# One reduction in place of three adds behind the attention's products with v, and another order of the work

## The chip, the cores and the metric

The kernel runs on one core of a Trainium2 chip. The metric is the device time in microseconds of one execution. TensorE (PE) does the matrix products, VectorE (DVE) and ScalarE (ACT) the arithmetic around them, GpSimd (POOL) helps out and issues some DMAs, SyncE (SP) issues the others.

## The reference

2048 tokens of width 640 go through two branches, which a gate for each token mixes. All arrays are fp32.

```python
qkv = (x @ wqkv)                       # 32 heads of 20 for q, k and v
idx = pos[:, None] - arange(8) * 2     # each token looks at itself and 7 earlier ones, 2 apart
logits = einsum("bhsd,bhswd->bhsw", q, k[idx]) * scale   # -1e9 where idx < 0
o = einsum("bhsw,bhswd->bhsd", softmax(logits), v[idx])
a = o @ wo
b = mish(x @ w1 + b1) @ w2             # inner width 1728
g = sigmoid((x * gate_w).sum(-1))
out = g * a + (1 - g) * b
```

## The kernel before

**Products.** Each fp32 product is done as three matrix products of a high part and a low part (`mm3`, L357 to L359). An operand is loaded into a buffer (`raw` or `hb`), ScalarE copies its high part (L322) and a subtraction makes its low part (L325); both stand in a `pair`. `qkv` makes q, k and v, `mlp1` the first product of the second branch with Mish on ScalarE, `mlp2` the second one as seven smaller products of sums of blocks, and `wo_out` the last product and the sum of both branches (L932). The sums of blocks of w2 are made by `sums_of_w2` (`sum_of`, L682), those of the activations by DMAs that GpSimd issues and that add to what stands in memory (`plus`, L591).

**Attention.** The heads are taken in four groups of eight, the tokens in two halves, which gives eight units. In a unit a partition holds 16 consecutive tokens, eight of each parity, so that the tokens 2 apart lie side by side along its row. Two tokens of each partition are done at a time, four times for each unit, so 32 times in all. `scores` multiplies q with the eight places of k (L402; 2 x 8 x 160 products in `pr`) and sums over the 20 elements of each head (L405). The softmax is split up over `softmax` (L418, L419, the exponential on ScalarE) and `shares` (L424 to L427). In the first tokens GpSimd adds a mask (`bounded`, L412). `outputs` multiplies the shares `pw` with the eight places of v into the same `pr` (L433) and sums over the eight places with three adds: 4 + 4 places (L437, 1280 elements), 2 + 2 (L438, 640) and 1 + 1 (L440, 320), the last one into the place of q. `out` turns the result (L365) and sends it to memory for `wo_out`. Each VectorE step of the attention follows the one before it, over all eight units.

**Order.** A planner (`Plan`) writes out the order by hand. Each step is a task with an engine, a cost in ns, a rank (a lower one goes first) and what it waits for; the planner plays the program with these costs, and the order in which it starts the tasks is the order of the instructions on each engine. `CARE` stretches the costs of an engine in that play, and `late` lets a task be ready only so much later than what it waits for. On the chip nothing of these times is left; only the order is, with the waits between the engines.

A task of the engine `"ANY"` (low halves, sums of w2, the gate's products) is shared: VectorE or GpSimd does it. While the attention goes on, GpSimd may start a task of rank 0 or more only if it ends, by its planned cost, at most 150 ns after the sum over the elements of a head (`kind` "qk sum"); the accumulating DMAs and the masks have a negative rank and may start at any time. A GpSimd instruction so placed gets a wait on the VectorE instruction ahead of that sum (`follow`). VectorE takes a shared task in the phase of the scores only when it has been ready for more than 2000 ns (`PATIENCE`), and in the phase of the outputs at once.

Of the kernel before, what the change touches and what calls it, by code (L numbers as in the profile page):

```python
# [10 lines left out]
AF = mybir.ActivationFunctionType  # L11
OP = mybir.AluOpType
AX = mybir.AxisListType
# [45 lines left out]
class Plan:  # L59
# [1 line left out]

    LAG = {"PE": 220, "ACT": 220, "DVE": 200, "POOL": 150, "SP": 3000}
    ADDING = 6000
    CARE = {"DVE": 1.015, "ACT": 1.1}

    def __init__(self, rings, follow):
        self.rings = {k: Ring(n) for k, n in rings.items()}
# [24 lines left out]
    def run(self):  # L92
        ready = {e: [] for e in self.LAG}
        busy = dict.fromkeys(self.LAG, False)
        events, n, left, wire = [], 0, len(self.tasks), 0.0


        quiet, gate, last, shared, phase, begun = 0.0, None, None, [], "", False
        loud = sum(t.kind != "" for t in self.tasks)
        for i, t in enumerate(self.tasks):  # L100
            t.key = (t.rank, i)
            t.rdy = 0.0
            if not t.waits:
                (shared if t.both else ready[t.eng]).append(t)
        now = 0.0

        def fits(t):
            want = {}
            for b in t.take:
                want[b.ring] = want.get(b.ring, 0) + 1  # L110
                if b.ring.free < want[b.ring] or b.ring.line[b.ring.at + want[b.ring] - 1] is not b:
                    return False
            return True

        while left:
            again = not events or events[0][0] > now
            while again:
                again = False
                for e in self.LAG:
                    if busy[e]:  # L120
                        continue
                    fit = [t for t in ready[e] if fits(t)]
                    on = begun and loud
                    if e == "POOL":
                        fit += [t for t in shared if fits(t)]
                        if on:
                            fit = [t for t in fit if now + t.ns[0] <= quiet + 150 or t.rank < 0]
                    elif e == "DVE":
                        fit += [t for t in shared if fits(t) and (now - t.rdy > self.PATIENCE or phase != "qk" or not on)]
                    if not fit:  # L130
                        continue
                    t = min(fit, key=lambda t: t.key)
                    if t.both:
                        shared.remove(t)
                        t.eng = e
                    else:
                        ready[e].remove(t)
                    if type(t.ns) is tuple:
                        t.ns = t.ns[e == "DVE"]
                    for b in t.take:  # L140
                        b.ring.free -= 1
                        b.ring.at += 1
                        b.t = b.make()
                    t.start = now
                    ins = t.fn(e) if t.both else t.fn()
                    if e == "POOL" and on and quiet > now and gate and ins:
                        self.follow(ins, gate)
                    if e == "DVE":
                        if t.kind:
                            begun = True  # L150
                            loud -= 1
                            phase = t.kind[:2]
                        if t.kind == "qk sum":
                            quiet, gate = now + t.ns, last
                        last = ins or last
                    busy[e] = again = True
                    end = over = now + t.ns * self.CARE.get(e, 1.0)
                    heapq.heappush(events, (over, n, "idle", e))
                    if t.land:
                        wire = max(wire, end) + t.land  # L160
                        end = wire + (0 if e == "SP" else self.ADDING)
                    heapq.heappush(events, (end + self.LAG[e], n + 1, "done", t))
                    if e != "SP":
                        heapq.heappush(events, (over, n + 2, "own", t))
                    n += 3
            if not events:
                stuck = [(t.eng, t.rank, t.waits, getattr(t.fn, "__qualname__", "")) for e in ready for t in ready[e]]
                raise RuntimeError(f"nothing can go on at {now}, {left} left: {stuck[:20]}")
            now, _, what, x = heapq.heappop(events)
            if what == "idle":  # L170
                busy[x] = False
                continue
            if what == "ready":
                (shared if x.both else ready[x.eng]).append(x)
                continue
            if what == "done":
                left -= 1
                x.at = now
                for b in x.hold:
                    b.left -= 1  # L180
                    if not b.left:
                        b.ring.free += 1
                        if b.gone:
                            b.gone()
            for t in x.then:

                if (t.eng == x.eng and x.eng != "SP") != (what == "own"):
                    continue
                t.waits -= 1
                if not t.waits:  # L190
                    t.why, t.rdy = x, now
                    heapq.heappush(events, (now + t.late, n, "ready", t))
                    n += 1
        return now
# [3 lines left out]
def kernel(ctx: ExitStack, tc: tile.TileContext, x, wq, wo, w1, b1, w2, xt, gw, out):  # L198
    nc = tc.nc
    scale = DH ** -0.5  # L200
    V, G, A = nc.vector, nc.gpsimd, nc.scalar
# [39 lines left out]
    def act_ns(n):  # L241
        return 30 + 0.96 * n
# [7 lines left out]
    def either(eng, n):  # L250
        return dve_ns(n) if eng == "DVE" else (pool_ns(n), dve_ns(n))
# [4 lines left out]
    add = plan.add  # L256

    SOON, NEXT, LATER, LAST = 0.0, 1.0, 2.0, 3.0
# [8 lines left out]
    gate = keep.tile([128, 2, 8], F32)  # L267
# [23 lines left out]
    pr = at.tile([128, 2, W, QF], F32, name="pr")  # L291
# [97 lines left out]
    def attention(u, P, hq, ready, gates):  # L389
        kv, q, r = KV[UNIT[u]], Q[UNIT[u]], LATER  # L390
        prev = last_att[0]
        def step(eng, ns, fn, after=(), **k):

            nonlocal prev
            t = add(eng, ns, fn, [prev] + list(after), **k)
            if eng == "DVE":
                prev = t
            return t
# [30 lines left out]
        def outputs(s0):  # L429
            def mul():  # L430
                vw = window(kv, s0, 1)
                vw = bass.AP(tensor=vw.tensor, offset=vw.offset, ap=[list(d) for d in vw.ap[:3]] + [[DH, HQ], [1, DH]])
                V.tensor_tensor(pr.rearrange("p s w (h d) -> p s w h d", d=DH), vw,  # L433
                                pw[:, s0:s0 + 2, :, :, None].to_broadcast([128, 2, W, HQ, DH]), op=OP.mult)

            step("DVE", 2850, mul, rank=r, kind="pv")
            step("DVE", 1495, lambda: V.tensor_tensor(pr[:, :, 0:4], pr[:, :, 0:4], pr[:, :, 4:8], op=OP.add), rank=r)  # L437
            step("DVE", 855, lambda: V.tensor_tensor(pr[:, :, 0:2], pr[:, :, 0:2], pr[:, :, 2:4], op=OP.add), rank=r)  # L438

            step("DVE", 525, lambda: V.tensor_tensor(q[:, s0:s0 + 2], pr[:, :, 0], pr[:, :, 1], op=OP.add), rank=r)  # L440

        def out(s0):
            ot = plan.buf("ot", lambda: at.tile([128, QF // 32, 4, 32], F32, name="ot"))
# [145 lines left out]

    def plus(key, src, after, hold=(), rows=128):  # L590
        return add("POOL", 1200, lambda: G.dma_start(out=blk[key][:rows], in_=src(), accum_op=OP.add, max_dma_last_dim=2048), after,  # L591
                   rank=-0.5, hold=hold, size=rows * 4096)

    def mish(src, n, fc, tb, after, hold, late=0, home=None):

# [71 lines left out]
    def sums_of_w2(kc):  # L667

        a1, a2, apart, o1, o2 = [raw_buf() for _ in range(5)]
# [6 lines left out]
        d = [halves(0, a1), halves(1, a2), dma(lambda: apart.t[:, :256].rearrange("p (f c) -> p f c", f=2),  # L676
             lambda: w2[kc::KH, :, 256:384].rearrange("f p c -> p f c"), rank=0.5, take=[apart], size=131072)]

        def sum_of(to, x, y, op, after, n=256, take=()):
            def run(e):  # L680
                (t, i), (a, j), (b, k) = to, x, y
                return (V if e == "DVE" else G).tensor_tensor(t.t[:, i:i + n], a.t[:, j:j + n], b.t[:, k:k + n], op=op)  # L682

            return add("ANY", either("ANY", n), run, after, rank=NEXT, take=take, hold=[to[0], x[0], y[0]])

        def kept(c, n, b, i, after):
            return dma(lambda: s_d[kc][:, c:c + n], lambda: b.t[:, i:i + n], after, rank=0.5, hold=[b], size=n * 512)

        s1 = sum_of((o1, 0), (a1, 256), (a2, 256), OP.add, d[:2], take=[o1])
        s2 = sum_of((o1, 256), (o1, 0), (a1, 0), OP.subtract, [s1])  # L690
        s3 = sum_of((o2, 0), (a1, 256), (a1, 0), OP.subtract, [s2], take=[o2])
        s4 = sum_of((o2, 256), (o1, 256), (a2, 0), OP.subtract, [s3])
        m = add("ACT", act_ns(128), lambda: A.activation(apart.t[:, 256:384], apart.t[:, :128], AF.Copy, scale=-1.0), d[2:], rank=LATER, hold=[apart])
        q = sum_of((apart, 384), (apart, 0), (apart, 128), OP.add, [m, s4], n=128)
        if kc == KH - 1:
            s4 = add("POOL", 300, lambda: G.memset(o2.t[FR:, 256:], 0.0), [s4], rank=-1.0, hold=[o2])
# [354 lines left out]
```

## Time and profile before

| what | value |
| --- | --- |
| median of 3 timed runs | 639.13 us (638.26 to 640.82) |
| profiled execution | 645.26 us, of which the span from the first to the last instruction is 643.5 us |
| TensorE | busy 633.6 us (98%), 2805 matrix products, mean granted clock 0.996 |
| VectorE | busy 586.5 us (91%), 623 instructions |
| ScalarE | busy 262.9 us (41%) |
| GpSimd | busy 125.3 us (19%) |
| memory traffic | 210 GB/s over the span |

A group of instructions is shown with its line, engine and operation, what it writes and reads, shapes, count, busy time in us, mean time of one in ns, and the idle time of its engine just ahead of them with what ended it. A stage is shown with its bounds and length, the busy time of TensorE, of its weight loads, of VectorE, ScalarE and GpSimd (with instructions), the granted clock, the share of the DMA engines, and GB/s. A wait is shown as the waiting instruction, what it waited for, the sum in us, how often, and the longest.

### The profile page before, as it was taken

To read this page: it belongs to the slowest core of one execution; us is meant where nothing else is said; L and a number is where in the kernel's file an instruction comes from. 1 tells how busy PE (TensorE), PEld (TensorE's weight loads), DVE (VectorE), ACT (ScalarE), POOL (GpSimd) and SP (SyncE) were. 2 spreads that over 40 slices of the span, in tenths; PEclk is the share of its full clock that TensorE was granted. 3 is DMA by queue.
4 is the path that set the end of the run, shared out by engine and by line. 5 is a ranking of instruction groups with operands and counts; after the bars stand their busy time and mean duration, and the time that the engine had idled before them with its cause. 6 is when DMAs were issued, how large, how long until landed. Compare 5 with 4: busy or idle time off the path is not lost.

```text
span 643.5 us, 8494 instructions
## 1 busy us (share of the span) xinstructions
PE 633.6 (98%) x2805; PEld 526.9 (82%) x2805; DVE 586.5 (91%) x623; ACT 262.9 (41%) x557; POOL 125.3 (19%) x118
## 2 busy tenths in 40 slices
PE   9999999999999999999999999799999999999997
PEld 6888888888888888888888888588888888888886
DVE  6877949999999998999999799999999999999961
ACT  7661533334227232431622254374759326641000
POOL 2202300250120121122103220061000101042910
PEclk9999999999999999999999999899999999999999
DMA  9999997976961797588699955699899567773642
GB/s 317 373 279 133 227 242 202 279 224 203 255 173 36 232 293 141 108 229 198 125 248 239 191 111 160 187 303 257 281 328 321 163 202 252 227 243 87 206 174 81
DMA packets 91324, 137.27 MB, mean 213 GB/s; under 512 B 12128, under 2 KB 41184, under 8 KB 91216
## 3 DMA queue, kind: packets, MB, share of 16 engines
q1 hardware_dynamic: 83600, 122.83, 61.4%
q0 software_dynamic: 7680, 13.90, 15.9%
q8 instruction: 22, 0.36, 0.2%
q14 instruction: 22, 0.18, 0.1%
HBM read 77.11 MB, written 57.81 MB: 210 GB/s over the span
## 4 chain that ended last, share of the span: by engine, by line
PE 85%; DVE 7%; issue 4%; DMA 2%; POOL 1%; ACT 0%; DVEq 0%; SPq 0%; POOLq 0%
PE bank L358 28%; PE bank L359 28%; PE bank L357 28%; DVE pr L433 1%; DVE pair L325 1%; POOL actt L591 1%; DVE pr L437 1%; PE bank L488 1%; DVE lg L405 1%; DVE pr L402 1%; DMA raw<-act 1%; DVE pr L438 1%; DMA hb<-in_wq 0%; DMA act<-hb 0%; DVE pw L427 0%
## 5 line engine op out<-in xcount | busy, mean ns | idle before, releaser
L358 PE MATMUL bank<-pair 128*128 128x512 f32 (+1 forms) x476 | 184.6, 388 | 4.8 <-DVE pair L325 4.8
L357 PE MATMUL bank<-pair 128*128 128x512 f32 (+1 forms) x476 | 184.5, 388 | 0.0
L359 PE MATMUL bank<-pair 128*128 128x512 f32 (+1 forms) x476 | 184.3, 387 | 0.0
L358 PEld LDWEIGHTS bank<-pair 128*128 128x128 f32 x476 | 89.8, 189 | 22.5 <-DVE pair L325 5.2
L359 PEld LDWEIGHTS bank<-pair 128*128 128x128 f32 x476 | 89.8, 189 | 17.3
L357 PEld LDWEIGHTS bank<-pair 128*128 128x128 f32 x476 | 89.6, 188 | 17.2
L322 ACT ACTIVATE pair<-raw 128x512 fp32r<-128x512 f32 (+3 forms) x122 | 72.5, 618 | 71.4 <-DMA raw<-o 26.6
L433 DVE TENSOR_TENSOR pr<-kvq,pw 128x2560 f32<-128x2560 f32 x32 | 91.3, 2852 | 0.7
L402 DVE TENSOR_TENSOR pr<-kvq 128x2560 f32<-128x2560 f32 x32 | 90.1, 2815 | 1.8 <-DMA kvq<-kvq 1.5
L405 DVE TENSOR_REDUCE lg<-pr 128x128 f32<-128x2560 f32 x32 | 90.2, 2817 | 0.6
L325 DVE TENSOR_TENSOR pair<-raw,pair 128x512 fp32r<-128x512 f32 (+3 forms) x114 | 73.8, 675 | 2.8 <-ACT pair L322 2.7
L358 PE MATMUL bank<-pair,kvq 128*128 128x512 f32 (+1 forms) x188 | 72.6, 386 | 0.0
L359 PE MATMUL bank<-pair,kvq 128*128 128x512 f32 (+1 forms) x188 | 72.6, 386 | 0.0
L357 PE MATMUL bank<-pair,kvq 128*128 128x512 f32 (+1 forms) x188 | 72.6, 386 | 0.0
L357 PE MATMUL bank<-pair,w 128*128 128x512 f32 x182 | 70.8, 389 | 0.0
L358 PE MATMUL bank<-pair,w 128*128 128x512 f32 x182 | 70.8, 389 | 0.0
L359 PE MATMUL bank<-pair,w 128*128 128x512 f32 x182 | 70.8, 389 | 0.0
L603 ACT ACTIVATE hb<-bank,bias 128x512 f32<-128x512 f32 x52 | 35.2, 686 | 70.8 <-DMA actt<-hb 52.8
L591 POOL DMA_DIRECT2D actt<-hb x26 | 24.9, 969 | 139.8 <-DMA actt<-hb 107.8
L322 ACT ACTIVATE pair<-hb 128x512 fp32r<-128x512 f32 (+3 forms) x63 | 38.8, 616 | 30.8 <-DMA hb<-o 13.2
L437 DVE TENSOR_TENSOR pr<-pr 128x1280 f32<-128x1280 f32 x32 | 48.1, 1503 | 0.7
L591 POOL DMA_DIRECT2D actt<-actt x28 | 26.5, 956 | 112.7 <-DMA actt<-actt 59.1
(88 smaller groups left out, 812.2 us busy)
## 6 DMA issues: line engine op xcount, KB each, us to landing
actt<-hb SPq DMA_DIRECT2D x52, 256.0 KB, 5.3
act<-hb SPq DMA_DIRECT2D x38, 256.0 KB, 4.7
raw<-actt SPq DMA_DIRECT2D x32, 256.0 KB, 4.7
raw<-act SPq DMA_DIRECT2D x29, 256.0 KB, 4.5
actt<-hb POOLq DMA_DIRECT2D x26, 256.0 KB, 5.8
actt<-actt POOLq DMA_DIRECT2D x24, 256.0 KB, 5.6
hb<-actt SPq DMA_DIRECT2D x24, 256.0 KB, 4.5
kvq<-in_xt SPq DMA_DIRECT2D x16, 320.0 KB, 7.3
```

The source lines that it names most:

```text
L322: a = add("ACT", act_ns(n), lambda: A.activation(hi(), raw(), AF.Copy), after, rank=rank, take=take, hold=hold)
L325: return (V if e == "DVE" else G).tensor_tensor(lo(), raw(), hi().bitcast(F32), op=OP.subtract)
L357: nc.tensor.matmul(ps, ah, bh, start=first, stop=False, skip_group_check=more)
L358: nc.tensor.matmul(ps, ah, bl, start=False, stop=False, skip_group_check=more)
L359: nc.tensor.matmul(ps, al, bh, start=False, stop=last, skip_group_check=more)
L402: return V.tensor_tensor(pr, window(kv, s0, 0), q[:, s0:s0 + 2, None, :].to_broadcast([128, 2, W, QF]), op=OP.mult)
L405: V.tensor_reduce(lg_w[:, s0:s0 + 2], pr.rearrange("p s w (h d) -> p s w h d", d=DH), op=OP.add, axis=AX.X)
L433: V.tensor_tensor(pr.rearrange("p s w (h d) -> p s w h d", d=DH), vw, pw[:, s0:s0 + 2, :, :, None].to_broadcast([128, 2, W, HQ, DH]), op=O ...
L437: step("DVE", 1495, lambda: V.tensor_tensor(pr[:, :, 0:4], pr[:, :, 0:4], pr[:, :, 4:8], op=OP.add), rank=r)
L438: step("DVE", 855, lambda: V.tensor_tensor(pr[:, :, 0:2], pr[:, :, 0:2], pr[:, :, 2:4], op=OP.add), rank=r)
L591: return add("POOL", 1200, lambda: G.dma_start(out=blk[key][:rows], in_=src(), accum_op=OP.add, max_dma_last_dim=2048), after, rank=-0.5, ...
L603: a = add("ACT", 595, lambda: A.activation(to(it()), src(), AF.Mish, bias=bias[:n, fc:fc + 1]), after + [bias_in], rank=NEXT, take=[] if h ...
```

## The change

The three adds are replaced by one reduction over the eight places. For it, `pr` is read through a view with the places as the innermost dimension, where two neighbours lie 160 floats apart. Its planned cost is 2750 ns, and its kind is "pv sum".

In the planner, GpSimd may now place shared tasks beside both kinds of sums; VectorE takes a shared task only after 2000 ns in both phases. VectorE's planned costs are stretched by 1.045 in place of 1.015. In the play, the accumulating DMAs become ready 1500 ns later, the first sum of each block of w2 and the negation on ScalarE 2500 ns later.

```diff
-    CARE = {"DVE": 1.015, "ACT": 1.1}
+    CARE = {"DVE": 1.045, "ACT": 1.1}
...
                     elif e == "DVE":
-                        fit += [t for t in shared if fits(t) and (now - t.rdy > self.PATIENCE or phase != "qk" or not on)]
+                        fit += [t for t in shared if fits(t) and (now - t.rdy > self.PATIENCE or not on)]
...
                             loud -= 1
-                            phase = t.kind[:2]
-                        if t.kind == "qk sum":
+                        if t.kind[3:] == "sum":
                             quiet, gate = now + t.ns, last
...
             step("DVE", 2850, mul, rank=r, kind="pv")
-            step("DVE", 1495, lambda: V.tensor_tensor(pr[:, :, 0:4], pr[:, :, 0:4], pr[:, :, 4:8], op=OP.add), rank=r)
-            step("DVE", 855, lambda: V.tensor_tensor(pr[:, :, 0:2], pr[:, :, 0:2], pr[:, :, 2:4], op=OP.add), rank=r)
-
-            step("DVE", 525, lambda: V.tensor_tensor(q[:, s0:s0 + 2], pr[:, :, 0], pr[:, :, 1], op=OP.add), rank=r)
+
+            step("DVE", 2750, lambda: V.tensor_reduce(q[:, s0:s0 + 2], pr.rearrange("p s w f -> p s f w"), op=OP.add, axis=AX.X),
+                 rank=r, kind="pv sum")
...
         return add("POOL", 1200, lambda: G.dma_start(out=blk[key][:rows], in_=src(), accum_op=OP.add, max_dma_last_dim=2048), after,
-                   rank=-0.5, hold=hold, size=rows * 4096)
+                   rank=-0.5, hold=hold, size=rows * 4096, late=1500)
...
-        s1 = sum_of((o1, 0), (a1, 256), (a2, 256), OP.add, d[:2], take=[o1])
+        s1 = sum_of((o1, 0), (a1, 256), (a2, 256), OP.add, d[:2], take=[o1], late=2500)
...
-        m = add("ACT", act_ns(128), lambda: A.activation(apart.t[:, 256:384], apart.t[:, :128], AF.Copy, scale=-1.0), d[2:], rank=LATER, hold=[apart])
+        m = add("ACT", act_ns(128), lambda: A.activation(apart.t[:, 256:384], apart.t[:, :128], AF.Copy, scale=-1.0), d[2:], rank=LATER, hold=[apart], late=2500)
```

`sum_of` gets the argument `late` and hands it to `add`; the variable `phase` goes.

More of the change, by code (lines that the diff above doesn't have):

```diff
@@ L95, in run @@
         events, n, left, wire = [], 0, len(self.tasks), 0.0
-        quiet, gate, last, shared, phase, begun = 0.0, None, None, [], "", False
+        quiet, gate, last, shared, begun = 0.0, None, None, [], False
         loud = sum(t.kind != "" for t in self.tasks)
@@ L677, in sums_of_w2, with sum_of @@
              lambda: w2[kc::KH, :, 256:384].rearrange("f p c -> p f c"), rank=0.5, take=[apart], size=131072)]
-        def sum_of(to, x, y, op, after, n=256, take=()):
+        def sum_of(to, x, y, op, after, n=256, take=(), late=0):
             def run(e):
@@ L682, in run @@
                 return (V if e == "DVE" else G).tensor_tensor(t.t[:, i:i + n], a.t[:, j:j + n], b.t[:, k:k + n], op=op)
-            return add("ANY", either("ANY", n), run, after, rank=NEXT, take=take, hold=[to[0], x[0], y[0]])
+            return add("ANY", either("ANY", n), run, after, rank=NEXT, take=take, hold=[to[0], x[0], y[0]], late=late)
         def kept(c, n, b, i, after):
             return dma(lambda: s_d[kc][:, c:c + n], lambda: b.t[:, i:i + n], after, rank=0.5, hold=[b], size=n * 512)
-        s1 = sum_of((o1, 0), (a1, 256), (a2, 256), OP.add, d[:2], take=[o1])
+        s1 = sum_of((o1, 0), (a1, 256), (a2, 256), OP.add, d[:2], take=[o1], late=2500)
         s2 = sum_of((o1, 256), (o1, 0), (a1, 0), OP.subtract, [s1])
```

## The prediction

> **What bounds the kernel now.** I read the page first, for the busy shares and the costliest groups; then TensorE's waits and its timeline around the longest; then VectorE by stage, and last the rows of the instructions that are exchanged.
>
> ```profile
> span 643.5 us, 8494 instructions
> PE 633.6 (98%) x2805; PEld 526.9 (82%) x2805; DVE 586.5 (91%) x623; ACT 262.9 (41%) x557; POOL 125.3 (19%) x118
> ...
> PE bank L358 <- DVE pair L325: 4.8, 1, 4.8
> ...
> 400.00:440.00 40.00, 35.23 (x149) 28.68 (x148) 39.83 (x43) 23.92 (x38) 12.62 (x7) 0.96 0.83 239
> 440.00:480.00 40.00, 40.00 (x178) 33.14 (x177) 39.66 (x54) 22.80 (x40) 2.91 (x4) 1.00 0.93 292
> ...
> 407.85 0.39 PE L357 MATMUL bank<-pair 128*128 128x512 f32 x1
> 413.00 0.50 PE L358 MATMUL bank<-pair 128*128 128x512 f32 x1 [4.76 <-DVE pair L325]
> ```
>
> TensorE is busy for 98% of the span and loses time in the middle at one place alone: it ends a matmul at 408 us and waits 4.76 us for a low half (L325) that VectorE writes late; behind it the granted clock of the stage is 0.96. The stage from 400 us has 149 matmuls where the next one has 178 in the same 40 us: 29 fewer, at 40/178 = 0.225 us each, are 6.5 us. Everything that this change could win on TensorE is that hole. The profiled execution took 645.26 us, 1.76 us more than its span; without the hole it would be 645.26 - 6.5 = 638.8 us. The timed runs lie at 638.26 to 640.82 with a median of 639.13, about there, so most of them probably lack the hole (that is an inference; they have no trace). A difference of 0.5% (3.2 us), about what a measurement of this kernel can tell from no change, would need 635.9 us. The change takes no matmul away, so I see no room for that.
>
> VectorE is nearly as full:
>
> ```profile
> 0.00:40.00 40.00, 38.58 (x165) 30.40 (x166) 29.12 (x50) 27.20 (x59) 7.66 (x10) 1.00 1.00 333
> 0.00:120.00 120.00, 118.58 (x522) 97.50 (x523) 94.48 (x128) 55.96 (x120) 19.98 (x22) 1.00 1.01 252
> 120.00:604.84 484.84, 480.07 (x2131) 400.82 (x2131) 472.29 (x470) 205.65 (x435) 96.21 (x91) 1.00 0.74 209
> 604.84:643.50 38.66, 34.93 (x155) 28.58 (x153) 19.71 (x27) 1.27 (x2) 9.10 (x6) 0.98 0.44 151
> ```
>
> ```profile
> 604.00 0.83 DVE L365 STREAM_TRANSPOSE ot<-kvq 128x640 f32<-128x640 f32 x1
> ```
>
> The third busy column is VectorE's. The cut at 604.84 us is the end of the last transpose of the attention (L365); behind it lies only the product with wo, 38.66 us long and TensorE's. Up to that cut VectorE works 94.48 + 472.29 = 566.8 us and is idle 38.1 us: 10.9 in the first 40 us, 14.6 up to 120 us, and 12.6 in the 485 us after that, 2.6% of them. An instruction made longer there has no cover: the attention must be done before the tail begins, its VectorE steps each follow the one before, and between them VectorE writes the low halves that TensorE waits for.
>
> **The change part by part. The sum over the places.** Three adds go, one reduction comes, 32 times each.
>
> ```profile
> L405 DVE TENSOR_REDUCE lg<-pr 128x128 f32<-128x2560 f32 x32 | 90.2, 2817 | 0.6
> ...
> L437 DVE TENSOR_TENSOR pr<-pr 128x1280 f32<-128x1280 f32 x32 | 48.1, 1503 | 0.7
> ...
> L438 DVE TENSOR_TENSOR pr<-pr 128x640 f32<-128x640 f32 x32 | 27.3, 854 | 0.8
> L440 DVE TENSOR_TENSOR kvq<-pr 128x320 f32<-128x320 f32 x32 | 17.6, 551 | 0.8
> ...
> L419 DVE TENSOR_TENSOR lg<-lg,mx x16: 410/424/426, 67.1 to 545.8; 128x256 f32<-128x256 f32 x16
> ...
> L427 DVE TENSOR_TENSOR pw<-lg,sm x16: 630/648/1101, 76.5 to 585.6; 128x256 f32<-128x256 f32 x16
> ```
>
> What goes is 1503 + 854 + 551 = 2908 ns. What comes has no row. It reads 2560 elements as L405 does, which takes 2817 ns, but L405 reads them one next to the other, and the new one steps over 160 floats (640 bytes) from each element to the next, because the places lie 160 apart in pr and are made innermost. The lower bound is L405's row: 2817 ns, a gain of 91 ns. The upper bound comes from the only pair of rows that differ in their step alone: L419 and L427 both take 256 elements of lg and a broadcast factor, and L427 writes with a step of 8 floats (32 bytes) where L419 writes side by side. Medians 424 and 648 ns: 224 ns more for 256 elements, 0.875 ns each. On 2560 elements that is 2240 ns, 5.06 us in all; and if the sum paid a whole second L405 less its fixed part (L419's 424 ns for 256 elements against 2817 for 2560 leave 1.039 ns per element) it would be 2817 + 2660 = 5.48 us. I take 5.06: L427 is a write and this is a read, but its step is the row nearest in kind, and L405's row has no large step at all. The cost is then 5.06 - 2.91 = 2.15 us each, 32 x 2.15 = 69 us; the ends are -3 us (32 x 0.091) and +82 us (32 x 2.57).
>
> The Trainium skill, "SBUF — State Buffer", section on the DMA port swizzle, says that the memory has lines of 16 bytes, that an access needs at least two hits on a line to run at full rate, and that four fp32 is as far as one can step for free. The pair L427 and L419 agrees (0.875 ns more per element at 32 bytes); no run here shows it for a read.
>
> **GpSimd beside the new sum.** Shared subtractions may now run on GpSimd during it, and VectorE takes a shared one that has waited under 2 us in no phase of the attention.
>
> ```profile
> L682 POOL TENSOR_TENSOR raw<-raw x9: 467/736/1090, 60.8 to 141.1; 128x256 f32<-128x256 f32 x8, 128x128 f32<-128x128 f32 x1
> ...
> L325 POOL TENSOR_TENSOR pair<-raw,pair x8: 1012/1296/1739, 19.9 to 605.9; 128x512 fp32r<-128x512 f32 x6, 128x384 fp32r<-128x384 f32 x2
> L325 POOL TENSOR_TENSOR pair<-hb,pair x4: 1294/1301/3869, 419.8 to 593.1; 128x512 fp32r<-128x512 f32 x4
> L325 POOL TENSOR_TENSOR w<-raw,w x3: 1561/1917/3978, 24.7 to 128.1; 128x640 fp32r<-128x640 f32 x3
> ...
> L325 DVE TENSOR_TENSOR pair<-raw,pair 128x512 fp32r<-128x512 f32 (+3 forms) x114 | 73.8, 675 | 2.8 <-ACT pair L322 2.7
> ...
> L682 DVE TENSOR_TENSOR raw<-raw 128x256 f32<-128x256 f32 (+1 forms) x26 | 9.9, 385 | 7.5 <-DMA raw<-in_w 7.4
> ```
>
> Before, GpSimd did 9 + 8 + 4 + 3 = 24 of them, most beside the 32 sums of the first kind. As many again beside 32 sums of the second kind would take 24 operations of 385 to 675 ns, about 0.55 us, from VectorE: 13 us. Bounds: nothing, and 26 us (twice as many, since the planned 2750 ns hold two of 1.3 us).
>
> Does it slow the sum? Here is a first sum with GpSimd beside it, and a product with GpSimd beside it:
>
> ```profile
> 418.36 2.81 DVE L405 TENSOR_REDUCE lg<-pr 128x128 f32<-128x2560 f32 x1
> ...
> 418.57 1.29 POOL L325 TENSOR_TENSOR pair<-raw,pair 128x512 fp32r<-128x512 f32 x1 [7.28 <-DVE pair L706]
> 419.83 1.29 POOL L325 TENSOR_TENSOR pair<-hb,pair 128x512 fp32r<-128x512 f32 x1
> ...
> 592.04 3.81 DVE L433 TENSOR_TENSOR pr<-kvq,pw 128x2560 f32<-128x2560 f32 x1
> ...
> 593.13 3.87 POOL L325 TENSOR_TENSOR pair<-hb,pair 128x512 fp32r<-128x512 f32 x1
> ```
>
> Beside the reduction both keep their time (2.81 and 1.29); beside a product of two tensors VectorE takes 3.81 and GpSimd 3.87. The new sum is a reduction with one input, so I put the slowing at nothing; its upper bound is 3.81 - 2.81 = 1.0 us on some 20 sums, 20 us. The Trainium skill, "GPSIMD Engine Reference", key points, says the same of two SBUF inputs, and the two pairs above agree.
>
> The new wait is GpSimd's on the product ahead of the sum. Behind it queue the accumulating DMA issues (L591) and the small masks (L412), for which VectorE waits in turn:
>
> ```profile
> DVE mx L418 <- POOL lg L412: 6.9, 3, 3.5
> DVE w L325 <- ACT w L322: 6.1, 2, 5.9
> ...
> POOL actt L591 <- DMA actt<-hb: 124.6, 13, 33.4
> ```
>
> GpSimd already stands 124.6 us in front of L591 for its data, at 19% busy, so a wait of a product's length is covered for the DMAs. For the masks it would lengthen 6.9 us of waiting by up to a product (2.8 us) in a few units; I count it against the idle time that goes elsewhere.
>
> **More reserve.** The factor 1.045 and the delays (1500 and 2500 ns) change only which instruction stands where. Removed is nothing. A step put later costs nothing while its reader is further off: the sums of w2 and the accumulations are read in the second product, long after. They can close the hole (6.5 us) and VectorE's 7.5 us before L682, or open a hole of the same kind elsewhere (6.5 us).
>
> **The sum.** VectorE up to the cut: 566.8 + 69 - 13 = 622.8 us. Its idle time of 38.1 us stays in the first 40 us (10.9) and partly after: waits for ACT and DMA (6.1 and 7.5 among them) vanish when VectorE itself is late, so I take 15 us off, which leaves 23. That is 646 us; the tail adds 38.7, what lies around the span 1.8: **686 us** against 645.26 profiled. The hole is not subtracted: it is TensorE's, which would have dozens of microseconds of new ones, all for VectorE. In such a bound state I expect timed runs near the profiled one, 47 us above their median. By the bounds of this case: least 566.8 + 69 - 26 + 10.9 + 38.7 + 1.8 = 661; most 566.8 + 82 + 38.1 + 38.7 + 1.8 = 727, or 20 more with the slowing, which I hold for unlikely.
>
> **The rivals. The stepped read is free.** Then the reduction takes L405's 2.82 us, VectorE loses 3 + 13 = 16 us of work, and TensorE's own 638.8 us decides: no change. This is the rival on the other side; it decides if the new sum stays under about 3.3 us, since 32 x 0.4 us are the 13 us that GpSimd takes off. For it speaks that no row shows a read that its step slows down; against it the 0.875 ns of L427.
>
> **The read is free, but the order makes a hole.** A low half left for GpSimd waits up to 2 us longer, GpSimd for the product, and TensorE for it: one or two holes of 6.5 us more than the floor, 645 to 652 us. For it speaks that one such hole exists now, behind a low half; against it the added reserve.
>
> **GpSimd gets nothing more.** If masks and DMA issues fill the new places, the 13 us stay on VectorE: 699 us with the slow read. For it speaks GpSimd's long standing in front of L591, against it that 24 got through beside the first sums. It lies inside the forecast's own range.
>
> **How the numbers follow.** Slow stepped read: 0.62, with 686 us and a range of its own of 661 to 727. Free read, no change: 0.28. Free read and a hole: 0.08, slower. The last 0.02 is a gain I cannot place. Some of the second case (0.01) may fall just past the bound. So faster 0.03, same 0.27, slower 0.70. The range that holds 8 in 10 must take in both kinds: from 637.5, just under the floor, to 715, where the last 12 us of the slow case's bound, with every term at its worst, are left out.
>
> **What would show it.** The row of the new reduction is the whole question: near 5.1 us I am right in the main step, near 2.8 us wrong. With it: VectorE's idle time from 120 us to the last transpose near nothing; the last transpose near 645 us; TensorE's waits for L325 and for freed buffers of some 45 us in sum, with a granted clock under 1 in those stages; L325 and L682 on GpSimd near 48. If the reduction is slow and the time still near 640, then VectorE had slack that its busy column hides, and my sum fails there.

## The result and the profile after

The changed kernel takes 690.01 us (median of 6 runs, 687.74 to 692.76) against 639.27 us (638.26 to 640.82): 1.0793 times as long, 95% interval 1.0765 to 1.0821. The profiled execution took 688.89 us with a span of 687.1 us.

The head of the page and the costliest groups of VectorE:

```profile
span 687.1 us, 8448 instructions
PE 648.6 (94%) x2805; PEld 534.6 (78%) x2805; DVE 634.3 (92%) x528; ACT 259.7 (38%) x557; POOL 161.8 (24%) x149
...
L437 DVE TENSOR_REDUCE kvq<-pr 128x320 f32<-128x2560 f32 x32 | 155.7, 4867 | 0.7
L432 DVE TENSOR_TENSOR pr<-kvq,pw 128x2560 f32<-128x2560 f32 x32 | 90.3, 2822 | 0.6
L404 DVE TENSOR_REDUCE lg<-pr 128x128 f32<-128x2560 f32 x32 | 90.2, 2818 | 0.6
```

L437 is the new reduction. It reads as many elements as the sum over a head (L404) and takes 4867 ns where that takes 2818. The three adds took 2908 together, so each of the 32 sums costs 1.96 us more: 63 us.

VectorE by stage, cut at the end of the last transpose as before, and what TensorE waited for:

```profile
638.63 0.82 DVE L364 STREAM_TRANSPOSE ot<-kvq 128x640 f32<-128x640 f32 x1
...
0.00:120.00 120.00, 118.80 (x523) 97.81 (x524) 100.47 (x109) 58.69 (x125) 27.05 (x31) 1.00 0.92 253
120.00:639.42 519.42, 485.90 (x2091) 400.78 (x2090) 511.49 (x390) 199.11 (x430) 124.26 (x112) 0.96 0.70 193
639.42:687.10 47.68, 43.90 (x194) 36.03 (x192) 22.36 (x32) 1.90 (x3) 10.45 (x7) 1.00 0.43 145
```

```profile
PE bank L357 <- DVE pair L324: 15.9, 7, 4.5
PE bank L358 <- DVE w L324: 10.5, 1, 10.5
PE bank L357 <- POOL pair L324: 6.1, 2, 3.4
```

Up to the cut VectorE has 612.0 us of work in 639.4 us; between 120 us and the cut it is idle for 7.9 us of 519. TensorE waits ten times for a low half, 32.5 us in all, and its granted clock is 0.96 on the mean of that stage. It is also "busy" for 15 us more (648.6 against 633.6) with the same 2805 products, and the clock accounts for that: over the whole span the mean granted clock is 0.973 here and 0.996 before, and 648.6 x 0.973 and 633.6 x 0.996 are both 631 us.

GpSimd's part of the shared work:

```profile
L324 POOL TENSOR_TENSOR pair<-raw,pair 128x512 fp32r<-128x512 f32 (+3 forms) x17 | 24.0, 1419 | 122.1 <-DVE pair L324 54.1 <-ACT w L601 36.1 <-ACT pair L321 31.2
...
L680 POOL TENSOR_TENSOR raw<-raw 128x256 f32<-128x256 f32 (+1 forms) x22 | 15.3, 710 | 64.8 <-DVE raw L680 42.4 <-DMA raw<-in_w 16.7 <-issue 5.6
L324 POOL TENSOR_TENSOR w<-raw,w 128x640 fp32r<-128x640 f32 x6 | 12.2, 2040 | 42.5 <-DVE pw L426 13.8 <-ACT w L321 9.5 <-DVE pr L401 8.6
L324 POOL TENSOR_TENSOR pair<-hb,pair 128x512 fp32r<-128x512 f32 x6 | 10.2, 1705 | 24.1 <-DVE pair L324 10.7 <-DMA h<-w 6.7 <-DVE pw L426 5.8
...
L324 POOL TENSOR_TENSOR kvq<-raw,kvq 128x640 fp32r<-128x640 f32 x2 | 3.1, 1574 | 9.0 <-DVE pair L324 6.9 <-DVE hb L784 2.1
```

These are 17 + 22 + 6 + 6 + 2 = 53 low halves and sums of w2, where the kernel before had 24. So GpSimd does take more of the shared work, as the second part of the change intends.

### The profile page after: what moved, and what is told of

It reads as the page before. It is cut to its first block, busy times and chain, and to the rows that moved or that the text cites. A ratio compares the mean times of both kernels' runs of the same rounds, so it can differ in the third digit from the quotient of the medians.

```text
span 687.1 us, 8448 instructions
## 1 busy us (share of the span) xinstructions
PE 648.6 (94%) x2805; PEld 534.6 (78%) x2805; DVE 634.3 (92%) x528; ACT 259.7 (38%) x557; POOL 161.8 (24%) x149
## 4 chain that ended last, share of the span: by engine, by line
DVE 30%; PE 18%; DMA 6%; issue 5%; SPq 1%; ACT 1%; POOL 0%; DVEq 0%; POOLq 0%; ACTq 0%
DVE kvq L437 11%; PE bank L357 6%; PE bank L358 6%; PE bank L356 6%; DVE pr L432 5%; DVE pr L401 4%; DVE lg L404 4%; DVE pair L324 3%; DMA hb<-actt 2%; DMA raw<-actt 1%; DMA raw<-act 1%; DMA b<-hb 1%; SPq L330 1%; DVE pw L426 1%; DVE ot L364 1%
## 5 line engine op out<-in xcount | busy, mean ns | idle before, releaser
L357 PE MATMUL bank<-pair 128*128 128x512 f32 (+1 forms) x476 | 189.2, 398 | 22.1 <-DVE pair L324 15.9
L358 PE MATMUL bank<-pair 128*128 128x512 f32 (+1 forms) x476 | 188.2, 395 | 0.0
L356 PE MATMUL bank<-pair 128*128 128x512 f32 (+1 forms) x476 | 188.0, 395 | 0.0
L437 DVE TENSOR_REDUCE kvq<-pr 128x320 f32<-128x2560 f32 x32 | 155.7, 4867 | 0.7
L357 PEld LDWEIGHTS bank<-pair 128*128 128x128 f32 x476 | 92.0, 193 | 44.1 <-DVE pair L324 19.2
L356 PEld LDWEIGHTS bank<-pair 128*128 128x128 f32 x476 | 92.1, 193 | 18.3
L358 PEld LDWEIGHTS bank<-pair 128*128 128x128 f32 x476 | 91.9, 193 | 17.9
L432 DVE TENSOR_TENSOR pr<-kvq,pw 128x2560 f32<-128x2560 f32 x32 | 90.3, 2822 | 0.6
L404 DVE TENSOR_REDUCE lg<-pr 128x128 f32<-128x2560 f32 x32 | 90.2, 2818 | 0.6
L324 DVE TENSOR_TENSOR pair<-raw,pair 128x512 fp32r<-128x512 f32 (+2 forms) x105 | 67.0, 668 | 4.0 <-ACT pair L321 4.0
L324 POOL TENSOR_TENSOR pair<-raw,pair 128x512 fp32r<-128x512 f32 (+3 forms) x17 | 24.0, 1419 | 122.1 <-DVE pair L324 54.1
L589 POOL DMA_DIRECT2D actt<-actt x28 | 24.7, 914 | 96.3 <-DMA actt<-actt 44.0
```

Source lines behind the costliest of these rows:

```text
L324: return (V if e == "DVE" else G).tensor_tensor(lo(), raw(), hi().bitcast(F32), op=OP.subtract)
L356: nc.tensor.matmul(ps, ah, bh, start=first, stop=False, skip_group_check=more)
L357: nc.tensor.matmul(ps, ah, bl, start=False, stop=False, skip_group_check=more)
L358: nc.tensor.matmul(ps, al, bh, start=False, stop=last, skip_group_check=more)
L404: V.tensor_reduce(lg_w[:, s0:s0 + 2], pr.rearrange("p s w (h d) -> p s w h d", d=DH), op=OP.add, axis=AX.X)
L437: step("DVE", 2750, lambda: V.tensor_reduce(q[:, s0:s0 + 2], pr.rearrange("p s w f -> p s f w"), op=OP.add, axis=AX.X), rank=r, kind="pv sum")
```

## The experiments

Theory 1: the step of the read makes the reduction long, and VectorE, already full, hands the whole of it to the end. Theory 2, the rival: the new order (reserve, patience, GpSimd's waits) makes TensorE's holes. Theory 3: the wrong planned cost does.

**1. The same reduction, side by side.**

```diff
-  pr.rearrange("p s w f -> p s f w")
+  pr.rearrange("p s w f -> p s (w f)").rearrange("p s (f w) -> p s f w", w=W)
```

> The changed kernel with one edit: the reduction reads eight neighbouring products in place of eight that lie 160 apart, so it adds up the wrong ones; as many elements in and out, the same order. Theory 1 (the step of the read): each reduction falls from 4.87 us to the 2.82 us of the sum over a head, VectorE loses 32 x 2.05 = 66 us of work, TensorE's floor of 638.8 us decides again: 637 to 642 us. Theory 2 (the new order, GpSimd's waits and the longer patience make the holes): the reduction may get faster, the time stays above 660 us.

638.97 us, ratio 0.9997 (0.9988 to 1.0007). The reduction and TensorE's only waits over 0.1 us:

```profile
L437 DVE TENSOR_REDUCE kvq<-pr 128x320 f32<-128x2560 f32 x32 | 90.2, 2817 | 0.7
```

```profile
PE bank L303 <- DVE lg L299: 1.2, 1, 1.2
PE bank L486 <- ACT pair L321: 0.5, 1, 0.5
```

Nothing but the addresses of the read was changed (so the kernel adds up the wrong products). All 51 us are gone, the hole that the kernel before had at 408 us in its profile too, and what is left is TensorE's floor, the time of its products with almost no waiting (busy for 632.1 of 637.6 us). Theory 1 holds here and theory 2 falls: with a fast reduction the new order makes no hole of more than 0.5 us. This is what the prediction's first rival would have given.

**2. The three adds in the new order.**

```diff
-  step("DVE", 2750, ... V.tensor_reduce(...), rank=r, kind="pv sum")
+  step("DVE", 1495, ...); step("DVE", 855, ...); step("DVE", 525, ...)    # as before
```

> The changed kernel with the three adds put back in place of the reduction, with their own planned costs; the reserve of 1.045, the delays and the patience in both phases stay, and GpSimd is let in beside the first kind of sums alone, since the second is gone. Theory 1: as the kernel before, within 0.5% of it, 637 to 642 us; if the reserve closes the hole at 408 us, 638 to 639. Theory 2: most of the 51 us stay, above 660 us.

650.76 us, ratio 1.0185 (1.0169 to 1.0200). Theory 1 had said 637 to 642 and missed: the rest of the change isn't free by itself. TensorE has holes again, of the kind that the kernel before has:

```profile
PE bank L358 <- DVE kvq L324: 6.0, 1, 6.0
PE bank L356 <- ACT kvq L321: 2.4, 1, 2.4
```

That is 12 us where the changed kernel loses 51, and in the first experiment the same reserve, patience and delays cost nothing. Experiments 7, 8, 10 and 11 follow this up.

**3. The reduction alone**, in the kernel before: no new place for GpSimd, no new patience, reserve or delays.

```diff
-  step("DVE", 1495, ...); step("DVE", 855, ...); step("DVE", 525, ...)
+  step("DVE", 2750, ... V.tensor_reduce(q[:, s0:s0 + 2], pr.rearrange("p s w f -> p s f w"), ...), rank=r)
```

> The kernel before with the reduction alone (planned at 2750 ns); GpSimd is not let in beside it, no new reserve, no new delays. Theory 1: 32 x (4.87 - 2.91) = 63 us more work for VectorE and nothing given to GpSimd: 645 + 63 less some 15 us of its idle time, 685 to 700 us, a little above the 690 of the changed kernel. Theory 2: within 10 us of the kernel before.

709.57 us, ratio 1.1109 (1.1061 to 1.1158), 10 us above what theory 1 allowed.

```profile
L437 DVE TENSOR_REDUCE kvq<-pr 128x320 f32<-128x2560 f32 x32 | 155.2, 4850 | 0.7
```

The instruction costs the same (4850 ns), so the 19.6 us down to the changed kernel are what GpSimd's new places, the patience, the reserve and the delays give back together. The traces point to GpSimd's places: VectorE's low halves and sums of w2 take 140.1 us here and 124.2 in the changed kernel, 15.9 us of the 18.4 between the two spans. No run takes the four one by one with the slow reduction, so that split isn't shown.

**4. The true cost in the plan.**

```diff
-  step("DVE", 2750, lambda: V.tensor_reduce(q
+  step("DVE", 4900, lambda: V.tensor_reduce(q
```

> The changed kernel with the planned cost of the reduction at 4900 ns in place of 2750, about what it takes; the instruction is the same. GpSimd's places beside it grow from two to three operations. Theory 1 (VectorE is simply too full): its work stays but for some 10 to 20 operations more on GpSimd, 6 to 12 us, 675 to 690 us. Theory 3 (the wrong cost in the plan, by which TensorE stands in front of halves that come late, is most of the loss): below 660 us.

690.89 us, ratio 1.0815 (1.0799 to 1.0831): just above theory 1's range, and theory 3 falls.

```profile
PE 642.5 (93%) x2805; PEld 531.1 (77%) x2805; DVE 632.3 (92%) x514; ACT 274.2 (40%) x563; POOL 179.4 (26%) x163
...
PE bank L356 <- ACT kvq L780: 22.5, 1, 22.5
```

The planner now knows the time, GpSimd does more (62 low halves and sums of w2 against 53, busy 179.4 us against 161.8), and VectorE still has 632 us to do; its largest group of low halves shrinks from 105 to 99, but one takes 724 ns on the mean in place of 668. Over half of the waiting moves into one hole of 22.5 us.

**5 and 6. Which step costs, and what else.** In the fifth, eight steps take turns in the 32 reductions; in the sixth the reductions stand behind the end of the kernel before, first alone, then beside products on TensorE.

```diff
+  bass.AP(tensor=pr.tensor, offset=pr.offset, ap=[list(pr.ap[0]), [W * QF, 2], [1, QF], [k, W]])   # k floats between addends
```

> The changed kernel with eight steps between the eight addends, each used for 4 of the 32 reductions: 1, 2, 3, 4, 8, 32, 96 and 160 floats (4 to 640 bytes); all but the last add up the wrong products. Theory 1a (a step costs once it leaves a line of 16 bytes): 2.8 us at 1 and 2, more from 3 or 4 on, and 4.9 us, all alike, from 4 on. Theory 1b (the longer the step the dearer): growing from 2.8 at 1 to 4.9 at 160, with 8 and 32 in between. Theory 1c (any step but 1): 2.8 at 1 and 4.9 at all others.

> The kernel before, and behind its last instruction the same reductions by themselves, with steps of 1, 2, 3, 4, 8, 32, 96, 159 and 160 floats, four of each: two while TensorE, ScalarE, GpSimd and the DMAs are still, and two while TensorE alone does products of 512 columns back to back. In the changed kernel the reduction took 4.45 us in the one place where TensorE and ScalarE stood still and 4.87 to 4.99 beside full TensorE. Theory A (TensorE's reads slow the stepped read): at step 160 4.45 us in the first part and about 4.85 in the second; at step 1 2.82 in both. Theory B (it was chance or another engine): the same time in both parts.

The fifth took 676.82 us (one run). Its reductions, with steps of 1, 2, 3, 4, 8, 32, 96 and 160 floats on lines L444 to L458 in this order:

```profile
L452 DVE TENSOR_REDUCE kvq<-pr 128x320 f32<-128x2560 f32 x4 | 20.4, 5098 | 0.1
L458 DVE TENSOR_REDUCE kvq<-pr 128x320 f32<-128x2560 f32 x4 | 19.7, 4935 | 0.1
L456 DVE TENSOR_REDUCE kvq<-pr 128x320 f32<-128x2560 f32 x4 | 19.3, 4835 | 0.1
L454 DVE TENSOR_REDUCE kvq<-pr 128x320 f32<-128x2560 f32 x4 | 19.3, 4820 | 0.0
L450 DVE TENSOR_REDUCE kvq<-pr 128x320 f32<-128x2560 f32 x4 | 19.2, 4810 | 0.1
L448 DVE TENSOR_REDUCE kvq<-pr 128x320 f32<-128x2560 f32 x4 | 15.3, 3822 | 0.1
L444 DVE TENSOR_REDUCE kvq<-pr 128x320 f32<-128x2560 f32 x4 | 11.3, 2819 | 0.1
L446 DVE TENSOR_REDUCE kvq<-pr 128x320 f32<-128x2560 f32 x4 | 11.3, 2818 | 0.1
```

A step of 1 or 2 floats (8 bytes) is free, 3 costs 1.0 us, 4 (16 bytes) already the full 2.0, and longer ones cost about the same, but for 8 with 5.10 us. Theory 1a has the shape, with the edge between 8 and 16 bytes; 1b and 1c fall. The Trainium skill, "SBUF — State Buffer", section on the DMA port swizzle, has two hits on a line of 16 bytes as the condition for full rate. That agrees: with 1 or 2 floats the addends lie two or more to such a line, and the reduction takes 2.82 us. On the same page the Trainium skill has four fp32 as how far one can step for free. That does not agree: 3 and 4 floats took 3.82 and 4.81 us in place of 2.82. The sixth, with the steps of 159, 160, 2 and 8 floats (L1022, L1023, L1016, L1019), first alone, then beside TensorE:

```profile
661.31 4.72 DVE L1022 TENSOR_REDUCE pw<-pr 128x320 f32<-128x2560 f32 x1
666.07 4.45 DVE L1023 TENSOR_REDUCE pw<-pr 128x320 f32<-128x2560 f32 x1
...
673.41 2.82 DVE L1016 TENSOR_REDUCE pw<-pr 128x320 f32<-128x2560 f32 x1
...
684.63 4.72 DVE L1019 TENSOR_REDUCE pw<-pr 128x320 f32<-128x2560 f32 x1
...
737.02 5.01 DVE L1022 TENSOR_REDUCE pw<-pr 128x320 f32<-128x2560 f32 x1
742.06 4.86 DVE L1023 TENSOR_REDUCE pw<-pr 128x320 f32<-128x2560 f32 x1
...
749.81 2.82 DVE L1016 TENSOR_REDUCE pw<-pr 128x320 f32<-128x2560 f32 x1
...
761.38 5.08 DVE L1019 TENSOR_REDUCE pw<-pr 128x320 f32<-128x2560 f32 x1
```

Theory A holds: the read with the long step takes 4.45 us alone and 4.86 beside TensorE (4.45 and 4.88 when repeated), the one with 2 floats 2.82 both times.

**7 and 8. What made the hole in the second experiment.** The seventh takes a shared task at once again in the phase of the outputs, the eighth takes the reserve back.

```diff
# 7, against the second experiment
-  now - t.rdy > self.PATIENCE or not on
+  now - t.rdy > self.PATIENCE or phase != "qk" or not on
# 8, against the second experiment
-  CARE = {"DVE": 1.045, "ACT": 1.1}
+  CARE = {"DVE": 1.015, "ACT": 1.1}
```

> As the second experiment (three adds, new order, 650.76 us), but VectorE takes a shared task at once in the phase of the outputs, as the kernel before does; the reserve of 1.045 and the delays stay. Theory 2a (the 12 us come from VectorE's patience of 2 us in a phase in which GpSimd is not let in): 638 to 642 us. Theory 2b (they come from the reserve or the delays): 646 to 652 us.

> As the second experiment, but VectorE's costs are stretched by 1.015 again; the patience in both phases and the delays stay. Theory 2a: still 646 to 655 us. Theory 2b, if it is the reserve: 638 to 642 us.

653.69 us (ratio 1.0234, 1.0219 to 1.0249) and 638.83 us (0.9996, 0.9987 to 1.0005). Theory 2a falls. Of 2b's two causes it is the reserve: taken back alone, with patience and delays kept, it brings the time down to the floor. The seventh lies above 2b's own range of 646 to 652 us, so taking shared tasks at once made the order slightly worse, for a reason that no run shows. In the eighth only the start is left:

```profile
PE bank L303 <- DVE lg L299: 1.2, 1, 1.2
```

**9. Pairs side by side.** If two addends within 8 bytes are enough, the idea of the change can be had: the places stand in pairs, and the reduction runs over the pair and then over the four pairs.

```diff
+  two = pr.rearrange("p s w f -> p s (w f)").rearrange("p s (a f c) -> p s a f c", a=W // 2, c=2)
   # product: one instruction for each of the two tokens, out = two[:, s] as "a c (h d)"
-  pr.rearrange("p s w f -> p s f w"), op=OP.add, axis=AX.X
+  two.rearrange("p s a f c -> p s f a c"), op=OP.add, axis=AX.XY
```

> The changed kernel with another layout of the products: the places stand in pairs, the two of a pair side by side and the pairs 320 floats apart. The product is done in two instructions of 1280 elements (one for each token, planned at 3000 ns together), each writing with a step of 2 floats; the reduction runs over pairs and places and gives the reference's sum. By the steps of 1, 2, 3 and 4 floats (2.82, 2.82, 3.82, 4.81 us), theory 1d says that two addends within 16 bytes are enough: reduction 2.82 us, products 2 x 1.5 us, VectorE some 5 us above the first experiment and still under TensorE's floor: 638 to 640 us. Theory 1e (each jump to a far line costs, whatever lies beside): reduction 3.8 us or more, 650 to 670 us. If writing with a step of 2 floats costs as L427's 32 bytes do, the products take 2 x 2.6 us: 670 us or more.

638.77 us, ratio 0.9994 (0.9986 to 1.0003), from 12 runs.

```profile
L441 DVE TENSOR_REDUCE kvq<-pr 128x320 f32<-128x2560 f32 x32 | 90.1, 2816 | 0.6
...
L436 DVE TENSOR_TENSOR pr<-kvq,pw 128x1280 f32<-128x1280 f32 x64 | 94.9, 1526 | 0.6
```

Theory 1d holds: the sum takes 2816 ns with a jump of 320 floats behind each pair. Writing with a step of 2 floats costs little: 2 x 1526 ns against 2822 for the one product of the changed kernel (L432), which includes what a second instruction costs by itself. The change's aim is met and buys no time: TensorE's floor is under both kernels.

**10 and 11. The reserve.** The tenth is the ninth with 1.015, the eleventh the eighth with 1.03.

```diff
# 10, against the ninth
-  CARE = {"DVE": 1.045, "ACT": 1.1}
+  CARE = {"DVE": 1.015, "ACT": 1.1}
# 11, against the eighth
-  CARE = {"DVE": 1.015, "ACT": 1.1}
+  CARE = {"DVE": 1.03, "ACT": 1.1}
```

> The kernel with the pairs side by side (638.77 us) with VectorE's costs stretched by 1.015 in place of 1.045. Theory 2c (the reserve is needed once GpSimd works beside both kinds of sums): holes of some microseconds before TensorE, 642 to 655 us. Theory 2d (with VectorE this light any order that the planner writes is fine): 638 to 640 us.

> The three adds with the new order, patience and delays, stretched by 1.03, between 1.015 (638.83 us) and 1.045 (650.76 us). Theory 2e (a larger stretch costs steadily, since it asks for work later): in between, 642 to 647 us. Theory 2f (each value of the stretch gives another order, and one in a few has a hole, without a trend): 638 to 640 us, or again 650 and more.

648.17 us (1.0155, 1.0125 to 1.0184) and 641.85 us (1.0042, 1.0024 to 1.0060). Without the reserve the tenth has holes before low halves:

```profile
PE bank L357 <- DVE pair L324: 5.0, 2, 3.9
```

So with GpSimd beside both sums the reserve is needed (2c), with three adds it harms: 638.83, 641.85 and 650.76 us at 1.015, 1.03 and 1.045. That grows, as 2e says, but 641.85 lies under its range, and three values don't tell a trend from three different orders. Why a larger reserve opens a hole is open.

## Why the prediction was right

The forecast was 686 us, the slow read its first term, and 690.01 came. The mechanism is shown: the slow read alone makes the kernel slower (third experiment), and without it the time is back at TensorE's floor (first experiment). That the number came within 4 us is partly luck, since errors cancelled in the sum. Point by point:

**The read.** 5.06 us were taken from L427's write; 4.87 came, so the term is 63 us and not 69. Of the two neighbours, L427's row was the right one: 0.80 ns more per element on the read ((4867 - 2818) / 2560) against 0.875 on the write. That a read pays about what a write pays was an assumption; at L427's own step of 8 floats the fifth experiment's read took 5.10 us, close to the 5.06. The prediction had no term for TensorE's part in the price: alone the read would take 4.45 us (sixth experiment), so about 32 x 0.42 = 13 of the 63 us hang on TensorE running beside it.

**GpSimd.** 24 more operations were expected, 29 came. VectorE's low halves and sums of w2, six groups of its table added up, fell from 140.6 to 124.2 us: 16 us and not 13. That GpSimd would not slow the reduction was right. Of two reductions beside a full TensorE and an idle ScalarE, the one with 3.07 us of GpSimd's work took 4.89 us, the one with none 4.87:

```profile
111.31:116.20 4.89, 4.89 (x24) 4.14 (x23) 4.89 (x2) 0.00 (x0) 3.07 (x3) 1.00 0.37 98
217.38:222.25 4.87, 4.87 (x24) 4.01 (x23) 4.87 (x1) 0.00 (x0) 0.00 (x0) 1.00 0.00 0
```

One sentence was wrong: GpSimd's new wait is not on the product. `mul` in `outputs` returns nothing, so `follow` gets an earlier instruction; the waits on L426 and on low halves in the groups above show it. (In the ninth experiment `mul` returns its instruction, so there the wait is on the product.) An operation can then start beside a product and stand there, as this one at 227.8 us (median of its kind 1.57 us):

```profile
227.80 4.05 POOL L324 TENSOR_TENSOR w<-raw,w 128x640 fp32r<-128x640 f32 x1 [13.85 <-DVE pw L426]
```

**The sum.** Two errors cancelled. VectorE reached the last transpose after 612.0 us of work and 27.5 idle, at 639.4 us in place of 646. But the tail took 47.7 us in place of 38.7: the step "the tail adds 38.7" failed, because TensorE came to that point with 194 products left where it had 155 before. These 39 more, at the 0.225 us of the prediction, are 8.8 us. A sum with the right work and idle time but the old tail would have said 680.

**The holes.** 45 us of waits were expected, 33 came; the lower clock in the stages with holes added 15 us of "busy".

**The rivals.** The free read gives 638.97 us (expected 638.8). The free read with a hole made by the order was given 0.08. With the fast reduction there is no such hole (first and ninth experiment), but it is real: with three adds and the new reserve it costs 12 us. What the order adds to the holes beside the long reduction was not separated.

## What to carry to other kernels

Before one reduction replaces a chain of adds, look at how far apart its addends lie: in fp32, steps of 4 and 8 bytes kept the full rate here, and a layout in pairs was enough for that; with a step of 16 bytes or more the instruction took 1.7 to 1.8 times as long beside TensorE. An engine that is 97% full inside a stage passes such a difference on to the end, whatever its share of the span says, while a saving there buys nothing once another engine is at its floor. A planner's reserve belongs to one set of costs: measure it again with each change of them, since here the same value closed holes in one kernel and opened them in another.

## What the hardware showed that was not expected

A VectorE read with a long step is slowed by TensorE: 4.45 us alone, 4.86 beside products of 512 columns, while reads with a step of up to 2 floats stay at 2.82. The changed kernel had hinted at it: in the one reduction during which TensorE stood still (0.02 us busy), and the DMAs, ScalarE and GpSimd with it, it took 4.45 us.

```profile
281.96:286.41 4.45, 0.02 (x1) 0.00 (x0) 4.45 (x1) 0.00 (x0) 0.00 (x0) 0.77 0.00 0
```

So a duration for such an instruction from a run by itself would be 8% short in a kernel that keeps TensorE busy. Steps of 8 floats are slower than 32, 96 or 160 (5.10 us against 4.82 to 4.94), and so is a step of 159 in the sixth experiment (5.01 us against 4.86 for 160), so it isn't the short step as such; which property of the address decides that is open.
